# Weight conversion through PSUM, and a second load of R and K, in an RWKV-6 plus gated feed-forward kernel

## The chip, the cores and the metric

The kernel runs on one core of a Trainium2 chip, in one launch. The metric is the device time of that core in microseconds (us). A core has TensorE (PE, matrix multiplies, whose weight loads the profile lists as PEld), VectorE (DVE), ScalarE (ACT), GpSimd (POOL) and SyncE (SP), each with an instruction stream of its own that runs in order. Here SP only issues transfers (DMAs).

## The reference

Two parts follow each other. The first is a linear-attention recurrence over a sequence, for 4 batches and 8 heads of 48 channels, 768 positions long:

```python
for t in range(S):
    cur = np.einsum('bhd,bhe->bhde', u[None] * kt, vt)
    y[:, :, t] = np.einsum('bhd,bhde->bhe', rt, state + cur)
    state = wt[:, :, :, None] * state + np.einsum('bhd,bhe->bhde', kt, vt)
```

The second takes the 4 x 768 = 3072 rows of y, 384 wide, through a feed-forward block with 2048 hidden units:

```python
h = x @ w_in
sp = np.maximum(h, 0.0) + np.log1p(np.exp(-np.abs(h)))
g = h * erf(sp)
return (g @ w_out).astype(np.float32)
```

Everything is float32 but the two weight matrices, which arrive as 64-bit floats, so that the kernel itself has to turn each pair of 32-bit words into one float32.

## The kernel before, in words

**Steps.** The work is cut into 12 steps. A step is one chunk of 128 positions for two of the four batches; its first two steps (c = 0) have no earlier state to apply, the others have. Step s runs `attend(s)`: seven levels of a scan, then a tail. At level L, PE multiplies K against R in blocks (line 246, 64 or 32 matmuls as the profile counts them, into the PSUM tile `pp`), and then VectorE multiplies parts of R and K in place by products of the decays w (line 257, tile `in`), which the next level of PE waits for. What PE has computed is folded into the tiles `own` and `late` by VectorE (lines 262 and 266) and, at the last levels, by ScalarE (lines 272 to 277). Level 1 uses another copy of R and K, the tile `rk1`, in which every second position is multiplied by u. The tail transposes K (line 289), forms y in a PSUM tile of its own from state, `own` and `late` (lines 301 and 309), copies y to `xT` (lines 315 to 318, with the remaining 48 rows moved by six small DMAs, line 323, half from SP's queue and half from ScalarE's) and updates the state (lines 335 to 348).

**What lies between the levels.** After each level and in the tail there is a place at which `fill` puts a piece of feed-forward work of an earlier step into PE's stream: two pieces of `project` of step s-3 at places 1 to 4, two pieces of `hidden` of step s-1 at places 5 to 8. A piece of `project` is 8 matmuls and one of `hidden` 12, as the profile counts them. Steps 1 and 2 have no `project` work yet and take their `hidden` pieces from the table `ALONE`; step 0 has nothing to put there. There and in the first levels of step 1 a small matmul, `keep_busy` (line 232), is put in. In `hidden`, ScalarE copies h out of PSUM (line 379) and then runs Softplus and Erf over 128x2048 elements, each with a table load (lines 385 and 356); VectorE multiplies the result into h (line 360).

**Preparing the next step.** `prepare(s+1)` is a generator that is advanced once per level of step s. GpSimd multiplies all of K and all of R by `u_pair` (u in one half of the positions, 1 in the other) into `rk1` (line 189, two instructions of 128x1024), then builds the decay products of all levels (line 205, seven instructions from 512 elements wide down to 8). `rk1` has one buffer.

**Conversion of the weights.** `convert` handles 32 pieces of 128x384 (16 of `w_in`, 16 of `w_out`), each in four stages: a DMA of the 64-bit words (line 131, six buffers `words`), two ScalarE multiplies (line 144 makes `base` from the high words, line 146 makes `rest` from the low words; four buffers each in SBUF), a VectorE shift of `base` (line 153) and a VectorE and-or that puts the sign in (line 156), both in SBUF, and a GpSimd add of `base` and `rest` into the weight (line 160). A turn of the generator loads five pieces ahead, scales three ahead and joins the present one. The table `CONVERT` says how many turns are taken after which level, including the place in the tail: 4 in step 0, 13 in step 1, 9 in step 2, 6 in step 3.

**Order.** The block is under a manual schedule: PE, VectorE, ScalarE and GpSimd run their instructions in the order in which the program emits them. SP's order is the tile framework's. `rk1`, `late`, `own`, `kT` and `y` have one buffer each; `in` has two.

Of the kernel before, what the change touches and what calls it, by code (L numbers as in the profile page):

```python
# [17 lines left out]
P = 128  # L18
EP = 64
HC = 64  # L20
NJ = 2
# [28 lines left out]
def kernel(  # L50
# [49 lines left out]
    y = ps_y.tile([P, NE, NJ, NP // 2, C], FP32, name="y")  # L100

    loaded = {}

# [15 lines left out]
    def convert(weights):  # L119


        held = {}

        def load(i):
            dst, src = weights[i]
            if src.dtype == FP32:
                nc.sync.dma_start(out=dst, in_=src)
                return
            n = dst.shape[1]
            words = wide.tile([P, n, 2], I32, name="words", bufs=6)  # L130
            nc.sync.dma_start(
                out=words[:].rearrange("p n two -> p (n two)"), in_=src.bitcast(I32)
            )
            held[i] = [words]

        def scale(i):
            if i in held:
                words = held[i][0]
                low, high = words[:, :, 0], words[:, :, 1]
                base = wide.tile(list(low.shape), FP32, name="base")  # L140
                rest = wide.tile(list(low.shape), I32, name="rest")


                nc.scalar.mul(out=base[:], in_=high.bitcast(FP32), mul=2.0**-112)  # L144

                nc.scalar.mul(out=rest[:], in_=low.bitcast(U32), mul=2.0**-29)  # L146
                held[i] += [base, rest]

        def join(i):
            if i in held:  # L150
                words, base, rest = held.pop(i)
                bits = base[:].bitcast(I32)
                nc.vector.tensor_scalar(  # L153
                    out=bits, in0=bits, scalar1=3, scalar2=None, op0=ALU.logical_shift_left
                )
                nc.vector.scalar_tensor_tensor(  # L156
                    out=bits, in0=words[:, :, 1], scalar=-(1 << 31), in1=bits,
                    op0=ALU.bitwise_and, op1=ALU.bitwise_or,
                )
                nc.gpsimd.tensor_tensor(  # L160
                    out=weights[i][0].bitcast(I32), in0=bits, in1=rest[:], op=ALU.add
                )

        for i in range(-5, len(weights)):
            for ahead, stage in ((5, load), (3, scale), (0, join)):
                if 0 <= i + ahead < len(weights):
                    stage(i + ahead)
            if i >= -1:
                yield

# [9 lines left out]
    def prepare(s):  # L180


        in_t = loaded[s][0]
        rk1 = att.tile([P, 2, JP, C], FP32, name="rk1", bufs=1)
        parts = 1 if s else NJ
        for i in range(parts):
            n = slice(i * JP // parts, (i + 1) * JP // parts)
            for x, engine in ((1, nc.gpsimd), (0, nc.gpsimd if s else nc.vector)):
                engine.tensor_mul(  # L189
                    rk1[:, x, n].rearrange("p n (t two) -> p n t two", two=2),  # L190
                    in_t[:, x, n].rearrange("p n (t two) -> p n t two", two=2),
                    u_pair[:, x, n, None, :].to_broadcast([P, JP // parts, C // 2, 2]),
                )
                if parts == 1:
                    yield

# [3 lines left out]
        for level in range(1, LOG + 1):  # L200
# [6 lines left out]
            used += nb  # L207
            if level == 2:
                yield
        ready[s] = rk1, tots, tot  # L210
        yield

    def attend(s, xT, fill, aside):


# [20 lines left out]
        for level in range(1, LOG + 1):  # L236
            half, nb = 1 << (level - 1), JP * C >> level
            rk = rk1[:] if level == 1 else RK
# [14 lines left out]
            if s == 0 or s == 1 and level < 3:  # L253
                keep_busy()

            halves = view(RK, half, [[SLOT - half, 2], [2 * half, nb], [1, half]])
            nc.vector.tensor_mul(  # L257
                halves, halves, view(tots[level - 1], 0, [[1, 2], [2, nb], [0, half]])
            )
            got = pp[:].rearrange("p e n t -> p (e n) t")  # L260
# [59 lines left out]
        for kk in range(KT):  # L320
            n = D // KT
            for e, queue in enumerate((nc.sync, nc.scalar)):
                queue.dma_start(
                    out=xT[e * EP + D : (e + 1) * EP, kk, :],
                    in_=y3[e * EP + kk * n : e * EP + (kk + 1) * n, :],
                )
        aside(LOG + 1)
        fill()
# [107 lines left out]

    CONVERT = ((0, 0, 0, 1, 0, 1, 1, 1), (1, 1, 1, 2, 2, 2, 2, 2), (1,) * 7 + (2,), (2, 2, 2))

    ALONE = {1: (0, 0, 1, 1, 1, 1, 2, 2), 2: (0, 1, 1, 1, 1, 1, 1, 2)}

# [4 lines left out]
    load_step(0, NJ)  # L445
    for j in range(NJ):
        for x in range(2):
            nc.gpsimd.tensor_copy(out=u_pair[:, x, j * NP : (j + 1) * NP, x], in_=u_sb[:])
    for t in v0_bufs:
        nc.vector.memset(t[HC:], 0.0)  # L450
    with tc.manual_schedule(
# [16 lines left out]
        for s in range(n_steps):  # L468
# [3 lines left out]
            def aside(level):  # L472
                for _ in range(CONVERT[s][level - 1] if s < len(CONVERT) and level <= len(CONVERT[s]) else 0):
                    next(conversion, None)

# [81 lines left out]
```

## Time and profile before

| what | value |
|---|---|
| time, median of 3 runs | 713.26 us (712.66 to 714.85) |
| profiled execution: time | 711.31 us |
| profiled execution: span from first to last instruction | 709.5 us |
| mean granted PE clock | 0.983 |
| PE busy | 680.3 us, 96% |
| PEld busy | 503.3 us, 71% |
| VectorE busy | 293.2 us, 41% |
| ScalarE busy | 309.5 us, 44% |
| GpSimd busy | 165.6 us, 23% |
| DMA | 45.78 MB |

The profiled execution is one run; 1.8 us of its time lie outside the span. A busy PE is not PE at its peak, since the ends of matmuls are modelled and a slow clock also counts as busy. The page's tenths by 40 slices show where PE is not full; the waits and the timeline, asked for a stretch, tell which engine it waited for. A wait for several semaphores is put down to the one that came last.

### The profile page before, as it was taken

Reading aid. Unit: us, or ns where it says so; the run is one execution under the profiler, and the core shown is the slowest. Engines: PE = TensorE matmul, PEld = TensorE weight load, DVE = VectorE, ACT = ScalarE, POOL = GpSimd, SP = SyncE. Lnnn points to the kernel's source line nnn. Section 1 sums busy time; section 2 is a strip of 40 time slices with the busy share of each in tenths; the row PEclk is TensorE's granted clock in tenths of the full one; section 3 lists DMA queues with packets and bytes.
Section 4 is the critical chain, followed back from the end, with each engine's and each line's share of the span. In section 5 each row is a group of like instructions: output and inputs, shape, how many; then the busy total and the mean of one; then the engine's idle time right before and its main releaser. Section 6 shows DMA issues by size and latency. Waiting matters only on the chain.

```text
span 709.5 us, 18369 instructions
## 1 busy us (share of the span) xinstructions
PE 680.3 (96%) x8458; PEld 503.3 (71%) x8458; DVE 293.2 (41%) x282; ACT 309.5 (44%) x387; POOL 165.6 (23%) x161
## 2 busy tenths in 40 slices
PE   8788889979999999999999999999999999999998
PEld 6566767648768768867867867867866866868654
DVE  6789585842442442352352262262262342210200
ACT  2237848605605704713722722632631641642700
POOL 5758273440320330240150050050050000000000
PEclk9899999989999999999999999999999999999999
DMA  8465624200300300300300300300210000000000
GB/s 315 146 209 163 218 69 161 81 12 13 130 12 13 129 13 13 129 13 12 128 3 24 106 24 24 106 26 24 92 39 24 4 5 24 5 3 23 1 22 22
DMA packets 15837, 45.78 MB, mean 65 GB/s; under 512 B 2832, under 2 KB 7184, under 8 KB 14352
## 3 DMA queue, kind: packets, MB, share of 16 engines
q1 hardware_dynamic: 14608, 44.02, 18.7%
q8 instruction: 66, 1.08, 0.6%
q10 hardware_dynamic: 1152, 0.59, 0.3%
q14 instruction: 11, 0.09, 0.0%
HBM read 38.70 MB, written 4.72 MB: 61 GB/s over the span
## 4 chain that ended last, share of the span: by engine, by line
PE 81%; ACT 6%; DVE 4%; issue 4%; DMA 3%; POOL 2%; SPq 0%; ACTq 0%; POOLq 0%; DVEq 0%
PE m L401 35%; PE m L372 31%; PE pp L246 9%; PE y L309 3%; DMA in<-in_rkw 2%; DVE in L257 1%; PE y L301 1%; PE pp L335 1%; ACT sp L356 1%; PE pp L289 1%; DVE base L153 1%; ACT sp L385 1%; DVE own L266 1%; DMA mask_sb<-in_masks 1%; ACT rest L146 1%
## 5 line engine op out<-in xcount | busy, mean ns | idle before, releaser
L372 PE MATMUL m<-xT,w_in_sb 128*128 128x256 f32 x1152 | 267.0, 388 | 2.8 <-ACT h L379 2.7
L401 PE MATMUL m<-w_out_sb,h 128*128 128x384 f32 x768 | 259.5, 493 | 4.3 <-POOL w_out_sb L160 4.3
L372 PEld LDWEIGHTS m<-xT,w_in_sb 128*128 128x128 f32 x1152 | 218.0, 193 | 35.5 <-POOL w_in_sb L160 1.7
L401 PEld LDWEIGHTS m<-w_out_sb,h 128*128 128x128 f32 x768 | 143.2, 190 | 99.7 <-POOL w_out_sb L160 6.0
L257 DVE TENSOR_TENSOR in<-in,tot_sb 128x1024 f32<-128x1024 f32 x72 | 93.8, 1303 | 211.9 <-PE pp L246 209.7
L360 DVE TENSOR_TENSOR h<-h,sp 128x1024 f32<-128x1024 f32 x48 | 64.6, 1387 | 112.1 <-ACT sp L356 112.1
L410 ACT COPY o<-m 128x384 f32<-128x384 f32 x24 | 11.5, 479 | 220.4 <-PE m L401 220.4
L246 PEld LDWEIGHTS pp<-in 48*64 48x64 f32 (+1 forms) x4224 | 71.4, 132 | 50.9 <-issue 25.4
L379 ACT COPY h<-m 128x512 f32<-128x512 f32 x96 | 55.5, 582 | 93.1 <-PE m L372 92.8
L246 PE MATMUL pp<-in 48*64 48x64 f32 (+1 forms) x4224 | 81.3, 219 | 14.4 <-DVE in L257 11.6
L189 POOL TENSOR_TENSOR rk<-in,u_pair 128x1024 f32<-128x1024 f32 (+1 forms) x24 | 54.0, 2264 | 69.0 <-PE pp L246 58.9
L345 POOL TENSOR_TENSOR s<-s,tot_sb 128x384 f32<-128x384 f32 x8 | 6.7, 831 | 233.4 <-PE y L301 233.4
L205 POOL TENSOR_TENSOR tot_sb<-tot_sb 128x256 f32<-128x256 f32 (+2 forms) x72 | 50.8, 705 | 5.4
L356 ACT ACTIVATE sp<-sp 128x2048 f32<-128x2048 f32 x24 | 45.9, 1911 | 0.3
L385 ACT ACTIVATE sp<-h 128x2048 f32<-128x2048 f32 x24 | 45.9, 1911 | 0.3
L266 DVE COPY_PREDICATED own<-mask_sb,pp 128x512 f32<-128x512 int32 x48 | 40.7, 849 | 0.0
L144 ACT ACTIVATE base<-words 128x384 f32<-128x384 f32 x32 | 17.8, 556 | 41.5 <-POOL w_in_sb L160 18.1
L356 ACT ACT_TABLE_LOAD x24 | 30.8, 1283 | 0.4
L385 ACT ACT_TABLE_LOAD x24 | 30.8, 1283 | 0.4
L160 POOL TENSOR_TENSOR w_out_sb<-base,rest 128x384 int32<-128x384 int32 x16 | 18.5, 1158 | 43.2 <-DVE base L156 31.3
L156 DVE SCALAR_TENSOR_TENSOR base<-words,base 128x384 int32<-128x384 int32 x32 | 27.5, 858 | 1.1
L257 DVE TENSOR_TENSOR in<-in 128x1024 f32<-128x1024 f32 x12 | 27.4, 2283 | 0.3
(45 smaller groups left out, 331.6 us busy)
## 6 DMA issues: line engine op xcount, KB each, us to landing
in<-in_rkw SPq DMA_DIRECT2D x11, 1536.0 KB, 7.4
words<-in_moe_w_in SPq DMA_DIRECT2D x16, 384.0 KB, 4.3
words<-in_moe_w_out SPq DMA_DIRECT2D x16, 384.0 KB, 3.4
v<-in_v SPq DMA_DIRECT2D x12, 384.0 KB, 3.8
out<-o SPq DMA_DIRECT2D x24, 192.0 KB, 1.9
v<-in_v SPq DMA_DIRECT2D x12, 192.0 KB, 4.0
in<-in_rkw SPq DMA_DIRECT2D x2, 512.0 KB, 4.4
xT<-y SPq DMA_DIRECT2D x36, 16.0 KB, 3.9
```

Source lines behind the costliest of these rows:

```text
L156: nc.vector.scalar_tensor_tensor(out=bits, in0=words[:, :, 1], scalar=-(1 << 31), in1=bits, op0=ALU.bitwise_and, op1=ALU.bitwise_or,)
L189: engine.tensor_mul(rk1[:, x, n].rearrange("p n (t two) -> p n t two", two=2), in_t[:, x, n].rearrange("p n (t two) -> p n t two", two=2), ...
L205: nc.gpsimd.tensor_mul(new, pair[:, :, 0], pair[:, :, 1])
L246: nc.tensor.matmul(pp[s0 : s0 + m, e, n, :m], lhsT=rk[rows(e), 1, n, s0 : s0 + m], rhs=rk[rows(e), 0, n, t0 : t0 + m], start=True, stop=True,)
L257: nc.vector.tensor_mul(halves, halves, view(tots[level - 1], 0, [[1, 2], [2, nb], [0, half]]))
L266: nc.vector.copy_predicated(rights(own[:], half), rights(mask_sb[:, level - 1 : level, :].to_broadcast([P, NH, HC]), half), rights(got, half),
L356: nc.scalar.activation(sp[:], sp[:], AF.Erf)
L360: nc.vector.tensor_mul(h[:, part], h[:, part], sp[:, part])
L372: nc.tensor.matmul(ps[:, ff, :], lhsT=w_in_sb[:, g * FG + f + ff, kk * P : (kk + 1) * P], rhs=xT[:, kk, :], start=kk == 0, stop=kk == KT - 1,)
L379: nc.scalar.copy(h[:, f : f + FT, :], ps[:])
L385: nc.scalar.activation(sp[:], h[:], AF.Softplus)
L401: nc.tensor.matmul(ps[j][:], lhsT=gs[g][:, f, j * C : (j + 1) * C], rhs=w_out_sb[:, g * FG + f, :], start=g + f == 0, stop=g == NG - 1 and ...
```

## The change: what it does

Six edits come together.

1. The conversion's `base` no longer lies in SBUF: ScalarE writes it into the PSUM tile `y` (bank i modulo 2), VectorE shifts it there, and the and-or reads it from there and writes a new SBUF tile `bits`. Because `y` is also the output of the step's tail, `base` is made only at the level in which its piece is finished; only `rest` is still made three pieces ahead.
2. `begin` (the ScalarE multiply) is emitted right behind a level's PE instructions, `finish` (VectorE's two instructions, GpSimd's add, then the load five ahead and `rest` three ahead) behind the level's other work. No conversion is left in the tail; the table becomes 4, 12, 10 and 6.
3. For steps after the first, `rk1` is filled by a DMA of R and K (1 MB, on SP's queue), and GpSimd multiplies by u in place only the half of each that needs it: two instructions of 128x512 in place of two of 128x1024. They come after the decay products instead of ahead of them.
4. In step 0, VectorE's multiply of a level is cut in two, one instruction for each batch.
5. All six DMAs of `xT` go to SP's queue.
6. `ALONE[1]` becomes (0, 0, 1, 1, 2, 1, 2, 1), from (0, 0, 1, 1, 1, 1, 2, 2); the four copies of u into `u_pair` change their order.

PE's instructions keep their order but for the `hidden` pieces that edit 6 moves.

```diff
+    CONVERT = ((0, 0, 0, 0, 1, 1, 2), (2, 2, 2, 2, 2, 2), (2, 1, 1, 2, 1, 1, 2), (2, 2, 2))
...
-        def scale(i):
+        def round_off(i):
             if i in held:
...
-                nc.scalar.mul(out=base[:], in_=high.bitcast(FP32), mul=2.0**-112)
-
+                low = held[i][0][:, :, 0]
+                rest = wide.tile(list(low.shape), I32, name="rest")
                 nc.scalar.mul(out=rest[:], in_=low.bitcast(U32), mul=2.0**-29)
+                held[i].append(rest)
+        def begin(i):
+            if i in held:
+                high = held[i][0][:, :, 1]
+                base = y[:, i % NE].rearrange("p j q t -> p (j q t)")[:, : high.shape[1]]
+                nc.scalar.mul(out=base, in_=high.bitcast(FP32), mul=2.0**-112)
+                held[i].append(base.bitcast(I32))
+        def finish(i):
+            if i in held:
+                words, rest, base = held.pop(i)
+                bits = wide.tile(list(rest.shape), I32, name="bits")
                 nc.vector.tensor_scalar(
-                    out=bits, in0=bits, scalar1=3, scalar2=None, op0=ALU.logical_shift_left
+                    out=base, in0=base, scalar1=3, scalar2=None, op0=ALU.logical_shift_left
                 )
                 nc.vector.scalar_tensor_tensor(
-                    out=bits, in0=words[:, :, 1], scalar=-(1 << 31), in1=bits,
+                    out=bits[:], in0=words[:, :, 1], scalar=-(1 << 31), in1=base,
                     op0=ALU.bitwise_and, op1=ALU.bitwise_or,
                 )
                 nc.gpsimd.tensor_tensor(
-                    out=weights[i][0].bitcast(I32), in0=bits, in1=rest[:], op=ALU.add
+                    out=weights[i][0].bitcast(I32), in0=bits[:], in1=rest[:], op=ALU.add
                 )
-        for i in range(-5, len(weights)):
-            for ahead, stage in ((5, load), (3, scale), (0, join)):
-                if 0 <= i + ahead < len(weights):
-                    stage(i + ahead)
-            if i >= -1:
-                yield
+        for i in range(5):
+            load(i)
+        for i in range(3):
+            round_off(i)
+        done = 0
+        while True:
+            count = yield
+            count = min(count or 0, len(weights) - done)
+            for i in range(done, done + count):
+                begin(i)
+            yield
+            for i in range(done, done + count):
+                finish(i)
+                for ahead, stage in ((5, load), (3, round_off)):
+                    if i + ahead < len(weights):
+                        stage(i + ahead)
+            done += count
...
-        parts = 1 if s else NJ
-        for i in range(parts):
-            n = slice(i * JP // parts, (i + 1) * JP // parts)
-            for x, engine in ((1, nc.gpsimd), (0, nc.gpsimd if s else nc.vector)):
-                engine.tensor_mul(
...
+        if s:
+            nc.sync.dma_start(out=rk1[:], in_=rkw[s][:, 0:2])
+        else:
...
         ready[s] = rk1, tots, tot
         yield
+        for x in range(2 if s else 0):
+            part = rk1[:, x].rearrange("p n (t two) -> p n t two", two=2)[:, :, :, x]
+            nc.gpsimd.tensor_mul(
+                part, part, u_pair[:, x, :, x : x + 1].to_broadcast([P, JP, C // 2])
+            )
+            yield
...
+            aside(level)
+            parts = 1 if s else NJ
+            for j in range(parts):
+                nb = JP // parts * C >> level
...
-            for e, queue in enumerate((nc.sync, nc.scalar)):
-                queue.dma_start(
+            for e in range(NE):
+                nc.sync.dma_start(
...
-    CONVERT = ((0, 0, 0, 1, 0, 1, 1, 1), (1, 1, 1, 2, 2, 2, 2, 2), (1,) * 7 + (2,), (2, 2, 2))
-    ALONE = {1: (0, 0, 1, 1, 1, 1, 2, 2), 2: (0, 1, 1, 1, 1, 1, 1, 2)}
+    ALONE = {1: (0, 0, 1, 1, 2, 1, 2, 1), 2: (0, 1, 1, 1, 1, 1, 1, 2)}
```

## The prediction

> **What bounds the kernel now.** The tenths by slice show PE full from slice 11 on and not before, so I asked for PE in stretches, one per step. A step's border is where its first level (L246 on rk) starts. Columns: stretch, length, busy time of each engine with instructions in brackets, PE clock, DMA share, GB/s.
>
> ```profile
> 8.42:37.36 28.94, 22.51 (x536) 14.55 (x535) 21.49 (x21) 11.04 (x21) 20.80 (x23) 0.88 0.69 227
> 37.36:81.66 44.30, 37.40 (x624) 29.95 (x621) 36.67 (x42) 26.13 (x44) 26.26 (x22) 0.96 0.64 201
> 81.66:125.76 44.10, 37.64 (x652) 31.36 (x648) 31.37 (x36) 32.04 (x47) 20.97 (x19) 0.92 0.40 121
> 125.76:187.60 61.84, 57.54 (x717) 41.95 (x713) 30.04 (x30) 27.32 (x37) 15.32 (x16) 0.94 0.17 58
> 187.60:242.43 54.83, 54.83 (x716) 40.93 (x712) 20.89 (x18) 23.41 (x28) 11.46 (x10) 1.00 0.14 50
> ```
>
> From step 4 on PE has no gap and a full clock. Steps 0 to 3 leave it idle for 6.4, 6.9, 6.5 and 4.3 us, 24.1 together, and their clock is 0.88 to 0.96. All conversions run there. Only there can the change move the end. Without gaps at full clock, step 3 would take the 54.8 of step 4; step 2, which lacks 8 pieces of 2.69 (5.38 per two in the chain), 33.3; step 1, also without the state's matmuls (1.0), 32.3 plus 2.2 of keep_busy. Some 18 us are lost in steps 1 and 2 and 7.0 in step 3. The waits of PE for 8.42 to 187.6 name the causes (total, times, longest):
>
> ```profile
> PE pp L246 <- DVE in L257: 11.6, 13, 3.5
> PE m L401 <- POOL w_out_sb L160: 4.3, 1, 4.3
> PE pp L246 <- issue: 2.8, 3, 1.4
> PE m L372 <- ACT h L379: 2.4, 2, 1.6
> PE y L309 <- ACT late L277: 1.5, 1, 1.5
> ```
>
> So PE waits for VectorE's level product. The timeline of step 2 shows what holds VectorE (start, length):
>
> ```profile
> 88.22 1.90 POOL L189 TENSOR_TENSOR rk<-in,u_pair 128x1024 f32<-128x1024 f32 x1
> 88.41 1.93 DVE L153 TENSOR_SCALAR base<-base 128x384 int32<-128x384 int32 x1
> ...
> 91.46 4.55 DVE L360 TENSOR_TENSOR h<-h,sp 128x1024 f32<-128x1024 f32 x2 [0.53 <-ACT sp L356]
> 92.03 2.89 POOL L189 TENSOR_TENSOR rk<-in,u_pair 128x1024 f32<-128x1024 f32 x1
> ...
> 97.19 1.16 PE L246 MATMUL pp<-in 48*64 48x64 f32 x64 [3.51 <-DVE in L257]
> ```
>
> L153 takes 0.35 alone and 1.93 behind a GpSimd L189; L360 4.55 against 2.36 elsewhere. Then PE stands for 3.51 and afterwards runs 12 matmuls in 4.54 instead of 2.86.
>
> **What the Trainium skill says.** "SBUF — State Buffer", section Who interferes with whom: VectorE in a 2-port mode, or with two SBUF inputs while GpSimd reads, excludes GpSimd for the whole instruction; with one SBUF input outside those modes it does not. The pair at 88.2 agrees: L153 ends at 90.3, L189 at 90.1. "VectorE: DVE Perf Modes", section Why PSUM operands drop a tier: an operand in PSUM takes the 2-port mode away; its table of operation costs gives 120 cycles plus one per element at 0.96 GHz, an estimate of (120+384)/0.96 = 0.53 us for the shift, which no run here shows. "GPSIMD Engine Reference", section 2.1: about 2.5 cycles per element with two inputs, at 1.2 GHz 1.07 us for 512; the trace has 1.04 for L205 of that width. "TensorE: Matmul & The Clock Gate", section What's actually happening: after an idle window of about 3.4 us PE runs at half clock until it was busy for as long. The slow matmuls after 97.19 agree.
>
> **The change part by part.**
>
> *Shift and and-or through PSUM.* 32 shifts go from 18.4 us (mean 0.576, least 0.346) to 32 x 0.53 = 17.0, 32 and-ors from 27.5 (mean 0.858, least 0.557) to 32 x 0.56 = 17.9: each has one SBUF input left and no lock. Bounds of a pair: 0.9 (as now when alone) to 1.3; I take 1.1. GpSimd's adds (1.0 alone, up to 1.9 now) then run beside them.
>
> *GpSimd's u product.* 22 instructions of 2.35 become 22 of 512 elements: least 1.04 (L205), most 1.5 with the strided write; I take 1.1. GpSimd is free by 27 us, hidden from step 4 on, since PE has no gap there. In steps 0 to 3 it shortens the locks against L257 and L360.
>
> *The second load.* 11 x 1 MB on SP. From step 3 on the DMA share is 0.17 or less and it is issued after level 1, over 45 us before the use: nothing. In step 0 the DMAs are full (rates near 390 GB/s until 20 us) and `in` of step 1 lands at 21.6. Behind it lie v (0.6 MB) and the 1 MB: at 360 GB/s (v and one piece of words, 0.98 MB, landed 2.7 after it) about 26.2.
>
> *Step 0.* Cutting the level product lets PE start a level 0.3 earlier (2.57 apart now, 2.28 of PE work with keep_busy), some 2 us, but GpSimd's queue decides the end: `in` lands at 21.6, products 5.5 (now 2.02+0.61+3.16, from 26.44), u 2.2, first add 1.0: 30.3. Now that add ends at 30.4. The fifth `rest` on ScalarE waits for this add's buffer, and behind it stand the last two `base`, `late`, kT and xT. New is that PE's y waits for the shifts that use its bank: rest 0.55, base 2 x 0.55, two pairs to about 33.9, y 2 (PE then cold up to 3.5), state 0.9: level 1 of step 1 at 38.0, against 37.36. **Loss 0.6**, between a gain of 3 and a loss of 3.
>
> *Step 1.* Two conversions per level at levels 1 to 6. VectorE per level: 1.23 + 0.70 + 2 x 1.1 = 4.1, with gaps 4.4. PE has only 2.3 at levels 1 and 2 and 3.85 at 3 and 4. Idle: 2.6 + 2.1 + 0.6 + 0.6, and about 1 where the products (5.5 us on GpSimd) delay an add, so that a `rest`, and behind it the next `base`, comes late. From level 5 PE has the longer work, and the tail, now 71.3 to 81.7 with waits for ScalarE's h copies and cold matmuls from 64.4, has no conversions and no ScalarE DMA issues (2.1). 32.3 + 2.2 + 6.9, less 1.0 of keep_busy that fills a wait: 40.4 against 44.3. **Gain 3.9.**
>
> *Step 2.* Softplus and Erf (2 x 3.2) of the last `hidden` piece end about 6.2 after the border, and `base` for level 1 is queued behind them on ScalarE; VectorE's shift waits and with it the product of level 2, to 9.5. PE's level 3 then starts at 9.6 instead of 8.1 after the border, but level 4 at 15.0 instead of 15.5, since L360's stall goes, and level 5 at 20 instead of 21.1. The y bank costs 1.3 at level 7, about what `late` costs now. **Gain 1.0**; bounds -4 and +5.
>
> *Step 3.* The same wait for Softplus and Erf lies under 10.7 of `project`. The last w_out pieces are finished at level 3: by the same sum about 21 after the border, PE needs them at 18.3 to 19: 2.0 of waiting in place of 4.3, and 2.6 of cold matmuls (4 took 3.19, 64 took 1.96) are gone. **Gain 4.5.**
>
> xT's DMAs on SP (six times some 0.6 instead of three) land about 1.9 later; the first use is 4 places on: nothing. ALONE only moves PE work.
>
> Sum: -0.6 + 3.9 + 1.0 + 4.5 = 8.8. From the profiled 711.31 (span 709.5 and 1.8 around it) that is 702.5. The median of three is 713.26, 1.95 above that execution; 713.26 - 8.8 = 704.5, and I take **704**.
>
> **Rivals.**
>
> *ScalarE becomes the brake (slower).* `base` is no longer three pieces ahead, so every shift waits for ScalarE, and VectorE's in-order stream carries the wait to PE. Places: level 6 and 7 of step 1, level 1, 6 and 7 of step 2, level 1 of step 3, all behind Softplus and Erf. For it: ScalarE is busy 4.9 of 5 us from 65 to 80. Against it: pieces of 2.7 to 5.4 on PE cover most. If PE loses 3 at each of the six, 18 less the 8.8, and 4 that is counted already, is 5 slower: 718. It decides once the mean loss passes about 2 us.
>
> *The second load comes late (no change).* If it lands at 33 instead of 26, the first step loses 7 more, and 711.5 is left. For it: the stream is full up to then. Against it: nothing but 1 MB and v is ahead of it, and the DMAs stand at 25 to 30.
>
> *The clock stays full.* If no wait passes 3 us in steps 1 to 3, all the cold matmuls go as well, and steps 1 and 2 come within 4 of their floor: 694.
>
> **How the numbers follow.** Forecast 0.66, ScalarE 0.17, late load 0.09 (0.07 of it no change), clock 0.08. About 0.3% (2.1 us) is what a measurement of this kernel can tell from no change. Faster 0.66 + 0.08 + 0.02 = 0.76, same 0.07, slower 0.17. The range 696 to 715 holds the forecast with its step bounds and the late load, and leaves out most of the ScalarE case and half of the last.
>
> **What would show it.** Right: shifts of 0.5 with hardly any spread; PE's wait for the level product under 8 us in steps 0 to 3; the wait for w_out near 2; steps of about 29.5, 40.4, 43 and 57; 54.8 from step 4. Wrong: VectorE waiting for `base` for over 10 us, a PE wait at y for the shifts of several us, the u product waiting for its DMA past 30, or a step after the fourth that is not 54.8.

## The result, and the profile after

| what | before | changed |
|---|---|---|
| time, median of 4 runs | 713.58 us (712.66 to 714.85) | 723.41 us (721.37 to 725.41) |
| ratio to before, 95% interval | | 1.0136 (1.0102 to 1.0170) |
| profiled execution: span | 709.5 us | 723.6 us |
| mean granted PE clock | 0.983 | 0.973 |
| VectorE busy | 293.2 us | 275.8 us |
| GpSimd busy | 165.6 us | 128.8 us |
| DMA | 45.78 MB | 57.32 MB |

The changed kernel is 1.4% slower, where 704 us (1.3% faster) was forecast. VectorE and GpSimd are busy for 17 and 37 us less, and the end of the profiled execution came 14 us later all the same. The two profiled executions lie further apart (14.1 us in span) than the medians (9.8): the profiled one is the slowest of the four for the changed kernel and lies below the median for the kernel before. The tables by step show the profiled executions.

The changed kernel by stretch, one step to a line (stretch, length, busy time of PE, PEld, VectorE, ScalarE and GpSimd with instructions in brackets, PE clock, DMA share, GB/s):

```profile
8.48:40.10 31.62, 22.44 (x534) 14.13 (x534) 20.83 (x28) 10.30 (x19) 14.48 (x23) 0.89 0.75 246
40.10:85.16 45.06, 37.14 (x625) 29.84 (x621) 29.50 (x40) 28.52 (x49) 20.98 (x21) 0.96 0.62 209
85.16:137.81 52.65, 39.43 (x653) 33.07 (x649) 31.58 (x38) 32.30 (x46) 24.62 (x20) 0.84 0.46 142
137.81:201.55 63.74, 59.37 (x717) 43.12 (x713) 27.29 (x30) 27.97 (x37) 15.90 (x17) 0.92 0.17 59
201.55:256.38 54.83, 54.83 (x716) 40.93 (x712) 20.00 (x18) 23.40 (x28) 7.33 (x11) 1.00 0.20 70
```

| step | before | forecast | changed | forecast was off by |
|---|---|---|---|---|
| 0 | 28.94 | 29.5 | 31.62 | 2.1 |
| 1 | 44.30 | 40.4 | 45.06 | 4.7 |
| 2 | 44.10 | 43.1 | 52.65 | 9.6 |
| 3 | 61.84 | 57.3 | 63.74 | 6.4 |
| sum | 179.18 | 170.3 | 193.07 | 22.8 |

All of the loss lies in steps 0 to 3, most of it in step 2, whose clock fell to 0.84. From the border of step 4 to the end of the span it is 709.5 - 187.6 = 521.9 us before and 723.6 - 201.55 = 522.05 after: the second load and the DMAs of xT cost nothing there.

PE's waits in the changed kernel, steps 0 to 3 (engine, what it waited for; total, times, longest):

```profile
PE pp L271 <- DVE in L288: 14.1, 10, 4.4
PE pp L271 <- issue: 6.0, 3, 4.0
PE y L333 <- DVE bits L165: 5.4, 1, 5.4
PE m L434 <- POOL w_out_sb L169: 4.4, 1, 4.4
```

And the one of VectorE's that is new:

```profile
DVE y L162 <- ACT y L155: 20.7, 8, 4.1
```

Before, VectorE waited for `base` once, 1.0 us. Now it waits 20.7 us for it (L155 is `begin`, L162 the shift), and PE waits longer for VectorE's level product (L288, 14.1 against 11.6), 5.4 for the y bank, and still 4.4 for w_out. Step 2's timeline shows the chain (start, length, engine, line):

```profile
113.39 1.28 ACT L418 ACT_TABLE_LOAD   x1
114.68 1.91 ACT L418 ACTIVATE sp<-h 128x2048 f32<-128x2048 f32 x1
116.50 0.50 ACT L155 ACTIVATE y<-words 128x384 f32<-128x384 f32 x1
117.03 0.57 DVE L162 TENSOR_SCALAR y<-y 128x384 int32<-128x384 int32 x1 [3.48 <-ACT y L155]
...
120.59 1.91 ACT L389 ACTIVATE sp<-sp 128x2048 f32<-128x2048 f32 x1
122.40 1.03 ACT L155 ACTIVATE y<-words 128x384 f32<-128x384 f32 x2
...
123.47 0.57 DVE L162 TENSOR_SCALAR y<-y 128x384 int32<-128x384 int32 x1 [4.09 <-ACT y L155]
...
125.98 1.96 PE L333 MATMUL y<-in,s 48*48 48x128 f32 x32 [5.40 <-DVE bits L165]
```

At level 6 the multiply that makes `base` takes 0.50 us, but it is issued behind Softplus with its table load (113.39 to 116.5). VectorE stands for 3.48 in front of its shift. At level 7 the two `base` multiplies stand behind Erf; VectorE waits 4.09, does two pairs of shift and and-or, and only then is the y bank free: PE has stood for 5.40. The three groups of y matmuls that follow take 1.96, 1.95 and 1.92 us, where they take 1.09, 1.10 and 1.10 in base_early below, in which the wait is 1.4.

The other waits of VectorE for `base` lie in step 1 (1.96, 0.58, 0.20 and, behind a Softplus, 3.43) and at level 1 of steps 2 and 3, behind Softplus and Erf (3.52 and 3.45).

### The profile page after: what moved, and what is told of

It is laid out like the page before. It is cut to its first block, busy times and chain, and to the rows that moved or that the text cites. A ratio compares the mean times of both kernels' runs of the same rounds, so it can differ in the third digit from the quotient of the medians.

```text
span 723.6 us, 18401 instructions
## 1 busy us (share of the span) xinstructions
PE 683.2 (94%) x8458; PEld 505.3 (70%) x8458; DVE 275.8 (38%) x289; ACT 312.0 (43%) x387; POOL 128.8 (18%) x161
## 2 busy tenths in 40 slices
DMA packets 17421, 57.32 MB, mean 79 GB/s; under 512 B 3008, under 2 KB 7360, under 8 KB 14528
## 4 chain that ended last, share of the span: by engine, by line
PE 78%; ACT 3%; DVE 2%; POOL 1%; issue 1%; DVEq 0%; POOLq 0%; ACTq 0%
PE m L434 34%; PE m L405 29%; PE pp L271 9%; PE y L341 3%; PE y L333 2%; PE pp L321 1%; PE pp L368 1%; ACT sp L389 1%; POOL tot_sb L225 1%; DVE bits L165 1%; DVE y L162 1%; ACT sp L418 1%; ACT L389 1%; ACT L418 1%; POOL w_out_sb L169 0%
## 5 line engine op out<-in xcount | busy, mean ns | idle before, releaser
L288 DVE TENSOR_TENSOR in<-in,tot_sb 128x1024 f32<-128x1024 f32 (+1 forms) x78 | 92.9, 1195 | 220.4 <-PE pp L271 218.2
L271 PEld LDWEIGHTS pp<-in 48*64 48x64 f32 (+1 forms) x4224 | 72.0, 133 | 57.7 <-issue 31.3
L393 DVE TENSOR_TENSOR h<-h,sp 128x1024 f32<-128x1024 f32 x48 | 67.6, 1448 | 106.5 <-ACT sp L389 106.5
L271 PE MATMUL pp<-in 48*64 48x64 f32 (+1 forms) x4224 | 81.8, 221 | 20.1 <-DVE in L288 14.1
L146 ACT ACTIVATE rest<-words 128x384 int32<-128x384 uint32 x32 | 17.8, 557 | 40.3 <-DMA words<-in_moe_w_in 20.2
L225 POOL TENSOR_TENSOR tot_sb<-tot_sb 128x256 f32<-128x256 f32 (+2 forms) x72 | 33.7, 468 | 5.6
L233 POOL TENSOR_TENSOR rk<-rk,u_pair 128x512 f32<-128x512 f32 x22 | 26.4, 1214 | 30.9 <-DMA rk<-in_rkw 30.9
L169 POOL TENSOR_TENSOR w_out_sb<-bits,rest 128x384 int32<-128x384 int32 x16 | 22.9, 1435 | 46.4 <-DVE bits L165 41.8
L304 ACT COPY late<-own 64x1024 f32<-64x1024 f32 x12 | 12.5, 1042 | 34.4 <-DVE own L298 34.4
L162 DVE TENSOR_SCALAR y<-y 128x384 int32<-128x384 int32 x32 | 18.3, 573 | 21.2 <-ACT y L155 20.7
```

What stands on the lines that cost most here:

```text
L162: nc.vector.tensor_scalar(out=base, in0=base, scalar1=3, scalar2=None, op0=ALU.logical_shift_left)
L225: nc.gpsimd.tensor_mul(new, pair[:, :, 0], pair[:, :, 1])
L233: nc.gpsimd.tensor_mul(part, part, u_pair[:, x, :, x : x + 1].to_broadcast([P, JP, C // 2]))
L271: nc.tensor.matmul(pp[s0 : s0 + m, e, n, :m], lhsT=rk[rows(e), 1, n, s0 : s0 + m], rhs=rk[rows(e), 0, n, t0 : t0 + m], start=True, stop=True,)
L288: nc.vector.tensor_mul(halves, halves, view(tots[level - 1], 2 * j * nb, [[1, 2], [2, nb], [0, half]]),)
L393: nc.vector.tensor_mul(h[:, part], h[:, part], sp[:, part])
```

## The experiments

Names: A, ScalarE's `base`, no longer ahead, is the brake; L, the second load delays step 0; S, the split of step 0's level product (edit 4) does. All ratios are to the kernel before, with 95% intervals; it was run beside each kernel, with medians of 712.5 to 712.7, and a recorded ratio is not always exactly the quotient of the medians. The last four columns are the steps of the profiled execution, one for each kernel.

| kernel | median us | ratio | 0 | 1 | 2 | 3 |
|---|---|---|---|---|---|---|
| base_ahead | 713.34 | 1.0007 (0.9997 to 1.0018) | 31.1 | 45.2 | 45.1 | 60.2 |
| base_early | 709.81 | 0.9962 (0.9948 to 0.9976) | 30.6 | 42.8 | 45.4 | 59.1 |
| counts_step2 | 720.82 | 1.0106 (1.0076 to 1.0136) | 29.2 | 45.1 | 48.9 | 60.9 |
| early_counts | 711.10 | 0.9977 (0.9966 to 0.9988) | 31.3 | 42.6 | 48.4 | 54.8 |
| no_load_step1 | 722.97 | 1.0146 (1.0129 to 1.0164) | 29.6 | 45.2 | 52.7 | 63.7 |
| before_extra_load | 712.69 | 1.0005 (0.9992 to 1.0018) | 29.6 | 44.4 | 44.3 | 63.1 |
| before_split | 711.93 | 0.9989 (0.9968 to 1.0011) | 28.0 | 44.4 | 44.4 | 63.0 |
| early_whole | 705.45 | 0.9899 (0.9877 to 0.9922) | 26.2 | 43.0 | 45.4 | 59.1 |
| after_whole | 724.00 | 1.0151 (1.0118 to 1.0185) | 31.2 | 45.7 | 52.5 | 63.6 |
| ahead_whole | 713.12 | 0.9999 (0.9977 to 1.0021) | 28.2 | 45.2 | 46.3 | 61.8 |
| early_whole_mul | 712.86 | 0.9996 (0.9978 to 1.0013) | 29.1 | 43.3 | 46.6 | 61.7 |
| early_whole_counts | 706.57 | 0.9902 (0.9880 to 0.9925) | 28.2 | 42.8 | 49.9 | 54.8 |
| whole_shift2 | 705.70 | 0.9913 (0.9891 to 0.9936) | 27.4 | 42.7 | 43.8 | 59.2 |
| whole_shift8 | 706.13 | 0.9913 (0.9881 to 0.9946) | 27.4 | 42.9 | 45.1 | 59.2 |
| split_less | 709.98 | 0.9963 (0.9949 to 0.9977) | 29.8 | 43.6 | 45.4 | 57.9 |

### Is it the base? Two ways of having it in time

base_ahead is the changed kernel with edit 1 undone: `base` three pieces ahead, in SBUF.

```diff
         def round_off(i):
...
+                base = wide.tile(list(low.shape), FP32, name="base")
+                nc.scalar.mul(out=base[:], in_=high.bitcast(FP32), mul=2.0**-112)
                 nc.scalar.mul(out=rest[:], in_=low.bitcast(U32), mul=2.0**-29)
...
         def begin(i):
             if i in held:
-                base = y[:, i % NE].rearrange("p j q t -> p (j q t)")[:, : high.shape[1]]
-                nc.scalar.mul(out=base, in_=high.bitcast(FP32), mul=2.0**-112)
+                pass
...
```

> The changed kernel with edit 1 undone: base is again made three pieces ahead, into SBUF, and shifted there; the tables, the second load and everything else stay as changed. Theory A (base made just in time on ScalarE, behind Softplus and Erf, holds VectorE and then PE): VectorE's waits for base, 20.7 us in the changed kernel, go; PE's wait before y in step 2 (5.4) falls under 1.5; step 2 goes from 52.7 to 44 to 46, step 3 from 63.7 to 60 to 62; the time falls from 723 to 711 to 714. Theory B (GpSimd's new order, the second load and the counts of the table cost the time; the PSUM shift in itself helps): step 2 stays over 50 and the time is 722 or more, with shifts of up to 1.9 again.

base_early leaves `base` in PSUM, but emits the multiplies for the next level's pieces right behind the present level's `finish`, which puts them ahead of Softplus and Erf in ScalarE's queue. It also puts them ahead of the `rest` multiplies of later pieces.

```diff
-            count = yield
-            for i in range(done, done + count):
-                begin(i)
-            yield
+            count, following = yield
             for i in range(done, done + count):
                 finish(i)
...
+            for i in range(done + count, done + count + following):
+                begin(i)
+            for i in range(done, done + count):
+                if i + 3 < len(weights):
+                    round_off(i + 3)
...
```

> The changed kernel with base still in PSUM, but each level's base made one level sooner: right behind the and-or of the level before (or behind the copies of y in the tail), ahead of the Softplus and Erf that are put in between. Theory A: VectorE's waits for base fall from 20.7 us to under 6, step 2 goes to 45 to 47, the time to 712 to 716. Theory B: the waits move to other instructions and the time stays within 3 us of 723.

Undoing the edit takes 10.1 us off (723.41 to 713.34), having the multiply a level earlier 13.6 (to 709.81). In base_early VectorE's wait for `base` is 1.7 us over the whole span instead of 20.7, PE's for the y bank 1.4 instead of 5.4, and step 2 is 7.3 shorter. A is shown, in two ways. base_ahead keeps the other five edits and takes as long as the kernel before: together they bring nothing there. The steps of base_early (columns as before):

```profile
8.50:39.12 30.62, 22.27 (x534) 14.03 (x535) 22.02 (x28) 10.37 (x19) 15.63 (x23) 0.89 0.73 253
39.12:81.90 42.78, 36.90 (x624) 29.93 (x621) 30.15 (x40) 29.75 (x51) 20.30 (x21) 0.96 0.65 219
81.90:127.30 45.40, 37.68 (x653) 31.41 (x649) 31.23 (x38) 31.65 (x46) 20.34 (x20) 0.92 0.51 164
127.30:186.40 59.10, 56.60 (x717) 41.46 (x713) 27.27 (x30) 26.86 (x35) 15.09 (x17) 0.97 0.19 65
```

Beside it, base_ahead's and-or, by form, is still under the lock (mean 938 ns); in the changed kernel it takes 555, and the shift 573 (count, busy us, mean ns, idle time before and what ended it):

```profile
L164 DVE SCALAR_TENSOR_TENSOR base<-words,base 128x384 int32<-128x384 int32 x32 | 30.0, 938 | 1.1
```

```profile
L162 DVE TENSOR_SCALAR y<-y 128x384 int32<-128x384 int32 x32 | 18.3, 573 | 21.2 <-ACT y L155 20.7
L165 DVE SCALAR_TENSOR_TENSOR bits<-words,y 128x384 int32<-128x384 int32 x32 | 17.8, 555 | 2.5
```

### Moving the pieces instead

counts_step2 leaves the order alone and moves step 2's conversions off levels 6 and 7: `(2, 1, 1, 2, 1, 1, 2)` becomes `(2, 2, 2, 2, 2, 0, 0)` in `CONVERT`.

> The changed kernel with step 2's row of the table as (2, 2, 2, 2, 2, 0, 0) in place of (2, 1, 1, 2, 1, 1, 2): the same 10 pieces, none at levels 6 and 7, where Softplus and Erf stand ahead of base. Theory A: PE's wait before y in step 2 (5.4 us) and the slow y matmuls behind it (5.8 in place of 3.2) go, step 2 falls from 52.7 to 44 to 46, the other steps stay within 1, and the time is 714 to 717. Rival: the pieces moved to levels 2 to 5 hold VectorE there for as long; step 2 stays over 49 and the time over 720.

The y wait is gone, but step 2 came down only to 48.9. At level 1 VectorE still waits 3.52 for a `base` behind the Softplus and Erf at the step's start, and PE then 4.37 for the level product; the wait for the product at the level after it grows from 1.11 to 2.12, with three more pieces at the early levels. The median is 2.6 us below the changed kernel's, where the rival had foretold over 720 (the profiled execution, at 716.79, is the fastest of its four runs). Moving the pieces took a small part of the loss away, the order on ScalarE all of it. early_counts is base_early with `(2, 2, 2, 2, 2, 2), (2, 2)` for steps 2 and 3, so that w_out is complete earlier.

> base_early with step 2's row (2, 2, 2, 2, 2, 2) and step 3's (2, 2): all conversions end one level sooner. If the last wait for w_out (2.5 us in step 3, with the slow matmuls behind it) is what remains of the loss, step 3 goes from 59.1 to 55 to 56, step 2 gains at most 1.5, and the time is 706 to 708. Rival: step 2 pays it back (ScalarE and VectorE have no room for two more pieces): 709.5 or more.

Step 3 is 54.8 us, the length of a step without any wait: the w_out wait and the slow matmuls behind it are gone. Step 2 is 48.4 instead of 45.4, with waits of 4.69 for a level product and 2.6 for `late`. Nothing was won (711.10 against 709.81). The same rows without the split, early_whole_counts, gave 706.57, where early_whole has 705.45:

> Base a level earlier, step 0 as a whole, and the shared pieces dealt 2,2,2,2,2,2 in step 2 and 2,2 in step 3. With the split in place these rows took step 3 from 59.1 to 54.8 and gave 3 of it back in step 2 (45.4 to 48.4). The same here: 705.45 - 4.3 + 3.0 = 704, at most 706. Rival: step 2 pays all of it back and more, 707 or over.

Again step 3 is 54.8 and step 2 is 4.5 longer: with either table the conversions are paid, in step 2 or in step 3.

### Step 0: the load, or the split

In step 0 of the changed kernel PE stands for 3.97 us before the last 20 of the 64 matmuls of level 5, with no releaser shown ("issue"). Step 0 is also where the second load first joins full DMAs. no_load_step1 fills step 1's `rk1` by two ScalarE copies instead:

```diff
-            nc.sync.dma_start(out=rk1[:], in_=rkw[s][:, 0:2])
+            if s == 1:
+                for x in range(2):
+                    nc.scalar.copy(rk1[:, x], in_t[:, x])
+            else:
+                nc.sync.dma_start(out=rk1[:], in_=rkw[s][:, 0:2])
```

> The changed kernel, but rk1 of step 1 is filled by two ScalarE copies from the loaded R and K in place of the second load; from step 2 on the load stays. Theory L (1 MB more in the full DMA queues of the first 26 us keeps PE's own instruction stream waiting): the gap of 3.97 us in PE in step 0, for which no releaser is shown, falls under 1.2, step 0 goes from 31.6 to about 29.5 and the time from 723 to 720 to 721. Rival: the gap has another cause and stays over 3, step 0 stays within 0.7 of 31.6.

before_extra_load is the kernel before with one load of R and K of step 1 more, into a tile that nothing reads.

```diff
+        if s == 1:
+            spare = hid.tile([P, FG, UNIT], FP32, name="h")
+            nc.sync.dma_start(
+                out=spare[:].rearrange("p f t -> p (f t)"),
+                in_=rkw[s][:, 0:2].rearrange("p x n t -> p (x n t)"),
+            )
```

> The kernel before with one DMA more: R and K of step 1 (1 MB) are loaded a second time, at the place of the changed kernel's load in SP's queue, into a buffer that nobody reads. Theory L: PE shows a gap without releaser of over 2.5 us between 20 and 28 us, step 0 grows from 28.9 to 31 to 32 and the time by 2 to 3. Rival: no such gap, step 0 within 0.7 of 28.9, the time within 0.3%.

Without the load step 0 is 2.0 shorter, as L said, but 2.87 us of the gap stay and the time is that of the changed kernel; with the load and without the other edits there is no such gap and no loss. L falls; before_split below, which has no second load, shows the gap all the same. before_split is the kernel before with edit 4 alone, early_whole is base_early with edit 4 undone:

```diff
-            parts = 1 if s else NJ
+            parts = 1
             for j in range(parts):
```

> The kernel before with edit 4 alone: the level product of step 0 cut in two. Theory S: PE shows a gap without releaser of over 2.5 us in level 5 (0.9 in the kernel before), step 0 grows from 28.9 to 30 to 31. Rival: the gap stays under 1.2 and step 0 falls by 0.5 to 2.

> base_early with edit 4 undone: in step 0 VectorE's level product is one instruction again. Theory S (the split brings PE's gap without releaser in step 0, 3.7 us in base_early): the gap falls under 1.2, step 0 from 30.6 to 29.5 or less. Rival (the split only lets PE start earlier; the gap is not its doing): the gap stays over 2.5 and step 0 grows by 0.5 to 2.

The split brings the gap, in both surroundings. (Step 0 of before_split fell to 28.0 in spite of it, as the rival had it.) PE in step 0 of before_split (levels 2, 3, 4 and 5; in brackets what PE waited for):

```profile
12.06 1.16 PE L246 MATMUL pp<-in 48*64 48x64 f32 x64 [0.82 <-DVE in L262]
14.95 1.47 PE L246 MATMUL pp<-in 48*64 48x64 f32 x64 [0.67 <-DVE in L262]
17.97 1.16 PE L246 MATMUL pp<-in 48*64 48x64 f32 x64 [0.50 <-DVE in L262]
20.68 0.92 PE L246 MATMUL pp<-in 48*64 48x64 f32 x44 [0.50 <-DVE in L262]
25.29 0.88 PE L246 MATMUL pp<-in 48*64 48x64 f32 x20 [3.69 <-issue]
```

And levels 4 and 5 of early_whole:

```profile
17.50 1.16 PE L271 MATMUL pp<-in 48*64 48x64 f32 x64 [0.34 <-DVE in L287]
...
20.06 0.92 PE L271 MATMUL pp<-in 48*64 48x64 f32 x46 [0.35 <-DVE in L287]
21.84 0.56 PE L271 MATMUL pp<-in 48*64 48x64 f32 x18 [0.86 <-issue]
```

Two things differ. PE's wait for the level product is 0.50 to 0.82 with the split and 0.34 without: the halves let PE start no earlier, but later. And the stop before the end of level 5 is 3.69 instead of 0.86. What it costs depends on what else ends step 0: nothing in the kernel before (711.93), 4.4 us on base_early (709.81 to 705.45), all of it in step 0 (30.62 to 26.18; the other three steps agree within 0.2).

after_whole and ahead_whole are the changed kernel and base_ahead with edit 4 undone:

> The changed kernel with its fourth edit alone undone: step 0 projects and shares as a whole again, not batch by batch. If the split costs here what it cost with the base made a level earlier (709.8 against 705.45), this is 4 to 5 faster than the changed kernel: 718 to 720 us, TensorE's gap before the last 20 matmuls of step 0's level 5 falls from 4.0 to 1.2 or less, and step 0 is about 27 us instead of 31.6. Rival: the waits for the base swallow what step 0 gives, then 722 or more.

> The changed kernel with its first and fourth edits undone: base three pieces ahead in SBUF, step 0 as a whole; the second load, the product by u and the conversions beside levels stay. If the two costs add up, 713.3 - 4.4 = 709 us, so the edits that stay are worth about 4 us against the kernel before. Rival: they are worth nothing by themselves and the split costs nothing where the base is ahead, as with the kernel before, to which the split alone did nothing (711.9): then 713.

Both expectations failed and the rivals held: no gain at all. In after_whole PE is through level 5 some 4 us earlier, and then stands for the shifts that occupy its y bank, 3.61 where the changed kernel had 1.59, and the y matmuls behind are slow:

```profile
31.02 0.55 ACT L146 ACTIVATE rest<-words 128x384 int32<-128x384 uint32 x1 [2.90 <-POOL w_in_sb L169]
31.47 1.05 ACT L155 ACTIVATE y<-words 128x384 f32<-128x384 f32 x2
...
34.95 1.95 PE L341 MATMUL y<-own,v 128*48 128x64 f32 x32 [3.61 <-DVE bits L165]
36.69 1.92 PE L341 MATMUL y<-late,v 128*48 128x64 f32 x32
```

There is no Softplus in step 0. The two `base` stand behind a `rest` that waits 2.90 us for GpSimd's add; in early_whole they are ahead of that `rest`, start at 27.80, and PE's wait is 1.10. Of the 4.5 us by which after_whole reaches the y bank sooner, 2.0 go into the longer wait and 2.0 into the slower matmuls behind it. So undoing the split alone gains nothing: in the changed kernel a second path, through GpSimd and `base`, ends almost as late as the one with the gap. In ahead_whole step 0 is 3.0 shorter than in base_ahead, and steps 2 and 3 are 2.9 longer in that execution; why they are isn't settled. (Single executions differ here: step 3 took 61.8 in the kernel before and 63.0 in before_split, with the same code.)

### What the gap is

DMA queue 8, which the profile calls "instruction", brings 16 KB at a time. In the kernel before it makes 66 transfers, and PE executes 8458 matmuls and 8458 weight loads: 256 instructions to a transfer. The two stops of PE in step 0 of the kernel before are as far apart: 14 + 2 + 64 + 2 + 46 = 128 matmuls with as many weight loads (lines between left out):

```profile
15.61 0.46 PE L246 MATMUL pp<-in 48*64 48x64 f32 x14 [0.52 <-issue]
...
21.81 0.56 PE L246 MATMUL pp<-in 48*64 48x64 f32 x18 [0.86 <-issue]
```

The DMA view of base_early between 22 and 24 us, and that of early_whole between 18.5 and 21 (packets, MB, share of 16 engines):

```profile
q8 instruction: 1, 0.02, 3.4%
```

```profile
q8 instruction: 1, 0.02, 2.9%
```

In all traces without the split this transfer starts at 19.2 to 20.2 us, before PE comes to its stop; in all with the split at 21.9 to 23.9, after it. Wherever the stop is seen, with and without the split, PE resumes 1.3 to 1.6 us after the transfer has landed (it lands at 24.65 in the changed kernel, where PE resumes at 26.13, and at 20.5 in early_whole, where PE resumes at 21.84). So PE has run out of instructions and waits for them. The split puts more waits into PE's stream, and the stop comes before the last 20 matmuls instead of the last 18. Is it this position (F) or the split itself (S)? whole_shift2 and whole_shift8 add PE instructions to early_whole, split_less takes some from base_early:

```diff
-                keep_busy()
+                keep_busy(2 if s == 0 and level < 2 else 1)
```

Here the argument is the number of parts into which the 512 columns are cut; whole_shift8 has `level < 5` in the place of `level < 2`. split_less:

```diff
-            if s == 0 or s == 1 and level < 3:
+            if s == 0 and level > 1 or s == 1 and level < 3:
                 keep_busy()
```

> The whole level product of step 0 stays (base a level earlier, no split), but the keep_busy of step 0's level 1 is issued as two halves of 256 columns: two matmuls and two weight loads more in PE's stream, hardly any time. Theory F (position): PE stops where a 16 KB block of its instructions ends and waits for the transfer of the next one; the split puts four more instructions ahead of that place (it stops before the last 20 matmuls of level 5 instead of the last 18) and thereby loses the early transfer. Then the same four instructions without the split bring the gap back: 3 to 4 us before the last 20 matmuls of level 5, the second transfer of instructions starting at 22 or later instead of 19 to 20, time 708 to 710. Theory S (the split's own work or waits make the gap): the gap stays at about 0.9 before the last 20, 705 to 707.

> As before, with the keep_busy of levels 1 to 4 of step 0 in two halves: 16 PE instructions more ahead of level 5. Theory F: the stop moves with the count, to before the last 26 matmuls of level 5 (18 + 8); whether it is 0.9 or 3 to 4 us long is not foretold. Theory S: it doesn't move with the count, and stays before the last 18.

> The split kept (base a level earlier), and the keep_busy of step 0's level 1 left out, so that PE's stream has four instructions fewer ahead of level 5. Theory F: the stop is before the last 18 again and short, 0.9 to 1.2, the second transfer of instructions starts near 19 to 20, step 0 is 26 to 28, time 705 to 707. Theory S: 3 to 4 us remain, time about 709.8.

The stop moves with the count: before the last 26 in whole_shift8 (18 + 8), before the last 18 in split_less. It is the end of a block of instructions. But its position doesn't make it long: whole_shift2 shows no stop in level 5 (PE begins the level at 21.7, when the transfer has landed, at 21.0), and split_less keeps a long one. PE in level 5 of whole_shift8 and of split_less:

```profile
23.02 0.68 PE L274 MATMUL pp<-in 48*64 48x64 f32 x26 [1.71 <-issue]
```

```profile
24.75 0.80 PE L271 MATMUL pp<-in 48*64 48x64 f32 x18 [3.43 <-issue]
```

F holds for where PE stops, S for how long. What in the split makes the transfer start only after the stop stays open.

### Edits 1 and 3, singly and together

early_whole_mul is early_whole with edit 3 undone: no second load, GpSimd multiplies all of K and R ahead of the decay products.

```diff
-            nc.sync.dma_start(out=rk1[:], in_=rkw[s][:, 0:2])
+            for x in (1, 0):
+                nc.gpsimd.tensor_mul(
+                    rk1[:, x].rearrange("p n (t two) -> p n t two", two=2),
+                    in_t[:, x].rearrange("p n (t two) -> p n t two", two=2),
+                    u_pair[:, x, :, None, :].to_broadcast([P, JP, C // 2, 2]),
+                )
+                if x:
+                    yield
...
-        for x in range(2 if s else 0):
+        for x in range(0):
...
```

> Base a level earlier, step 0 as a whole, and the third edit undone: no second load and no product by u in place, R and K multiplied as in the kernel before. If the third edit is what brings the rest of the gain, this is 2 to 4 us slower than 705.45 (707.5 to 709.5), with longer VectorE operations beside GpSimd's in steps 1 to 3. Rival: the third edit is worth nothing, 704.5 to 706.5.

It is 7.4 us slower than early_whole, more than either expectation (by step 2.9, 0.4, 1.2 and 2.6). With the kernel before and ahead_whole this makes a square (median us; edits 2, 5 and 6 are in three of the four, not in the kernel before, and edit 4 in none; the right column has `base` in PSUM and its new place on ScalarE at once):

| | base ahead, in SBUF | base a level early, in PSUM |
|---|---|---|
| R and K multiplied whole | 712.6 (before) | 712.86 |
| second load, half multiplied | 713.12 | 705.45 |

Neither alone moves the time; together they take off 7. In step 3 of early_whole_mul, GpSimd's product and VectorE's level product meet, and w_out comes late:

```profile
143.07 2.88 POOL L206 TENSOR_TENSOR rk<-in,u_pair 128x1024 f32<-128x1024 f32 x1
144.11 2.92 DVE L296 TENSOR_TENSOR in<-in,tot_sb 128x1024 f32<-128x1024 f32 x1
...
149.94 2.93 PE L441 MATMUL m<-w_out_sb,h 128*128 128x384 f32 x4 [4.39 <-POOL w_out_sb L169]
```

In the same step a GpSimd product that comes first takes 1.90, and a level product with no GpSimd beside it 1.23. The level products of levels 2 and 3 take 2.57 and 2.92 here, 1.23 and 2.06 in early_whole, 2.2 us less together, and there the wait for w_out is 2.50. This agrees with what the Trainium skill states in "SBUF — State Buffer", section Who interferes with whom: a VectorE instruction with two SBUF inputs contends with a GpSimd instruction that reads SBUF, and the lock is exclusive. In ahead_whole the lock that stays is the and-or's (mean 918 ns against 555). How much of the 7 us each lock is worth in each step, and how much the place of `base` on ScalarE, was not measured.

## Why the prediction was wrong

**The step that failed** is the cover of `base`. The working of step 2 put the wait for the y bank at 1.3 us ("about what `late` costs now"). It measured 5.4, and the y matmuls behind it were slow for another 2.5, which the working put at nothing: 6.6 of the 9.6 by which step 2 was off. The working did see Softplus and Erf ahead of the `base` of level 1, and took none at levels 6 and 7 in the forecast, though the first rival listed those places. At level 6 the Softplus of the fourth `hidden` piece stands ahead of `base`; this delay pushes the copies of `own` and `late`, and with them Erf, into level 7's. With `base` a level early that wait is 1.4, as priced. The other 3.0 arose earlier, for the most part: from the border of the step, level 3 started at 10.9 (9.6 in the working), level 4 at 18.3 (15.0) and level 5 at 22.2 (20). PE in levels 3 and 4:

```profile
96.06 1.99 PE L271 MATMUL pp<-in 48*64 48x64 f32 x64 [4.37 <-DVE in L288]
97.97 4.35 PE L405 MATMUL m<-xT,w_in_sb 128*128 128x256 f32 x12
103.43 1.16 PE L271 MATMUL pp<-in 48*64 48x64 f32 x64 [1.11 <-DVE in L288]
```

Behind the wait of 4.37 the matmuls were slow for 2.3 us (1.16 and 2.86 elsewhere), which the working had not counted, and VectorE's two multiplies of the old L360 took 3.15, less than 4.55 but not the 2.36 of an undisturbed pair.

**The first rival is what happened.** It named six places and assumed that PE loses 3 us at each. One of them, level 7 of step 1, has no conversion in the new table; at the other five VectorE waited 3.4 to 4.1 each, 18.0 of its 20.7. For PE that came out as a few long waits and slow matmuls behind them, and the kernel ended above the rival's 718. Ten us of the loss go with the edit undone. Its counter-argument, "pieces of 2.7 to 5.4 on PE cover most", was the mistake: PE does the piece while ScalarE works, but VectorE then has the shifts, the and-ors and the level product still ahead, in order.

**Step 1** (gain 3.9, measured a loss of 0.8). Of the 4.7, the `base` costs 2.3 (45.06 to 42.78 in base_early). Most of the rest is slow matmuls taken as gone: in base_early 24 of `hidden` still take 7.11 us, as the 7.10 of the kernel before, where 24 that are not slow take 5.45. The losses of steps 1 and 2, "some 18" in the working, are 20.6 by its own floors (44.30 - 34.5 and 44.10 - 33.3); the forecast doesn't rest on this.

**Step 3** (gain 4.5, measured a loss of 1.9). The wait for w_out was taken as 2.0 and stayed at 4.37, with slow matmuls behind it, since VectorE waited 3.45 for the `base` of level 1. With `base` in time (base_early) PE's wait for w_out is 2.5 and little behind it is slow: the 64 matmuls of the next level take 1.29 and the 16 after them 5.43, against 1.99 and 7.49 in the changed kernel behind its wait of 4.37. These two waits agree with the idle window of about 3.4 us in the Trainium skill's "TensorE: Matmul & The Clock Gate", section What's actually happening. The 7.11 of step 1 does not follow from one such wait: it came behind 1.98 us, with shorter gaps before. Step 3 of base_early still is 59.1, not 57.3, since the four matmuls of the late piece take 2.93, waiting again for its second half. early_counts reached 54.8 and paid in step 2.

**Step 0** (loss 0.6, measured 2.7). The split was taken to let PE start each level 0.3 earlier; the levels came 0.15 to 0.5 later, and a stop of 4 us for instructions, which nothing in the working foresaw, was added. In the changed kernel the rest of the step follows upon this stop. The path that the working followed, from GpSimd's add over `rest` and `base` to the y bank, is the one that ends after_whole: there the two pairs end at 34.9, against 33.9, and the y matmuls take 3.9 (1.95 and 1.92), against 2 to 3.5. Luck helped the add: it ended at 30.64 (30.3 in the working), with the products begun at 23.1 instead of 21.6, over in 3.5 instead of 5.5, and 0.85 of waiting for the load.

**Right** were the prices of most operations: and-ors of 0.555 (0.56), the u product 1.06 in steps 0 to 3 (1.1 taken). The shifts took 0.573 with hardly any spread (0.55 to 0.67), near the 0.53 estimated, but their sum of 18.3 us is what it was before (18.4). The second load was no hindrance: GpSimd's first product by u starts at 27.4, against "about 26.2" and the rival's 33; SP's six DMAs cost nothing, and step 4 is 54.83.

Where `base` is in time and the split is gone (early_whole), the change gains 7.2 us, near the 8.8 forecast, but the nearness is luck. In the profiled executions step 0 gains 2.8, where a loss of 0.6 was forecast, and steps 1 to 3 gain 1.3, -1.3 and 2.8, where 3.9, 1.0 and 4.5 were.

## What to carry to other kernels

When a producer is moved from "three pieces ahead" to "when needed", its length is not its price: look up what is queued ahead of it on its in-order engine at that place, and follow the wait through the consumer's queue to the bound engine. Here the place in the program of one multiply, half a microsecond long, was worth 13.6 us. Two edits that each moved nothing alone took off 7 us together, so edits against the same exclusion between two engines should be tried together as well as singly.

Of the kernels run, early_whole (the change with `begin` a level earlier and step 0's product left whole) is the fastest: 705.45 us, 1.0% faster than the kernel before (ratio 0.9899, 0.9877 to 0.9922) where the changed one is 1.4% slower. whole_shift2, whole_shift8 and early_whole_counts can't be told from it: their intervals overlap with its own.

## What the runs showed of the hardware that was not expected

TensorE can run out of instructions: in these traces its stream comes in 16 KB transfers of 256 instructions, and at the end of a block PE stood for at most 1.7 us where the next transfer had started ahead of the stop, and for 2.9 to 4.0 where it started after it, with no releaser shown. A few more or fewer instructions move the place of this stop one for one, and a gap marked "issue" that falls inside a run of equal matmuls is worth a look at the instruction queue in the DMA view.

The same code of step 0 took 26.2 us in early_whole's profiled execution and 28.2 in early_whole_counts', with y matmuls of 1.10 in the one and 1.95 in the other, although the wait ahead of them was 1.10 in both; so a single profile does not price a slow clock to better than 2 us there.
